# Linear attention with a top-1 mixture of experts: four early expert tiles in place of two, the first with an unsplit fp32 first layer

## The chip, the cores and the metric

The kernel runs on one core of a Trainium2 chip. The metric is the device time of one execution in microseconds (us). The outputs are fp32 and come from fp32 inputs.

## The reference

Four batches of eight heads, 768 positions and 64 channels go through a linear attention that fades with `lam`, one rate a head; its output, seen as 3072 tokens of 512 features, goes through a mixture of eight experts of which each token takes one:

```python
for b in range(nb):                       # blocks of positions, per batch and head
    intra = einsum('bhic,bhjc->bhij', qb, kb) * Dmask
    intra = einsum('bhij,bhjd->bhid', intra, vb)
    inter = einsum('bhid,bhde->bhie', qb * lam_pow, kv_state)
    out[:, :, sl] = intra + inter
    kv_state = lam_block * kv_state + einsum('bhsd,bhse->bhde', kb * rev_pow, vb)
x = out.transpose(0, 2, 1, 3).reshape(3072, 512)
logits = x @ w_gate + modality_bias[modality_id]
e_idx = argmax(logits, axis=1)            # one of 8 experts
gate_w = softmax(logits)[e_idx]
out[mask] = gate_w[mask] * (relu(x[mask] @ w1[e]) @ w2[e])   # 512 -> 1024 -> 512
```

With the inputs used, expert 3 gets 1319 tokens, expert 5 253, expert 6 1494, expert 7 6, and the others none. After the first 1024 tokens the same four have 433, 87, 502 and 2, after the first 2048 they have 885, 164, 994 and 5.

## The kernel before, in words

**The attention.** The positions are taken in chunks of 128: 24 chunks, 6 for each batch, in 12 pairs (loop `for m in range(pairs)`). A pair's q, k and v come in one transfer of 2 MB (`load`, L88 and, for the first two pairs, L92) into one of six slots of 2 MB, which later serve the expert weights too: raw1 and raw2 (w1 and w2 of one expert as they arrive) and w1h, w1l, w2h, w2l (their high and low parts). For each chunk TensorE makes the scores (L253), VectorE masks them (L257), TensorE adds what comes from the state (L292) and from the values (L300), ScalarE copies the result out as xt (L303), VectorE transposes it (`turn`, L309), and a transfer on ScalarE's queue stores the rows in xs in device memory (L313). The state is three rotating tiles: POOL multiplies the old one by the fade (`fade`, L273), TensorE makes the new products kv (L265), VectorE adds both (`add`, L282). After every second pair, the gate matmuls (`gates`, L320) make the logits of four chunks.

**The routing.** It goes in three batches of 8 chunks (1024 tokens): `choose` (L340: the expert of each token, its weight), `ranks` (L364 to L367, matmuls that count each token's place in its expert's list), `slots_of`, and `write_slots` (L394: POOL's indirect transfers that write each token's number into the table inv in device memory). `count` adds up the tokens of each expert. All of the small VectorE instructions of these functions show line 340, that of the helper `put`; they are put on a list, and `do(n)` issues the next n of them.

**The experts.** Tiles of 256 tokens of one expert ("wide"), and two "thin" tiles of 64 and 32 tokens for remainders. `early_list` chooses two full tiles from the first 1024 tokens (listA); the rest follows from `late_list` (listB), with at least MIN_WIDE = 10 wide tiles. For a tile, SP fetches its piece of inv (`fetch_idx`: found, idx, L559 to L567), VectorE makes row indices of it (`spread_idx`, gidx, L575), POOL gathers the rows with indirect transfers (`fetch_rows`, xg, L585), VectorE turns them (`turn_rows`, xt, L610), and ScalarE and VectorE split x and the weights into a high part (L543) and a low part (L544). `fetch_w1` and `fetch_w2` (L600, L605) fetch the weights of the tile's expert in four transfers each. A product of split operands is three F32R matmuls (`three`, L622 to L624). The first layer goes in four blocks of 24 matmuls; after each block ScalarE takes hh (L643) and VectorE hl (L644). The second layer is two halves of 24 matmuls of 512 columns; its result y goes out by an indirect transfer (L658). A thin tile isn't split: its two layers are plain fp32 matmuls (L674 and L701), with transposes between (L685 and L687).

**The order.** TensorE, VectorE, ScalarE and SP issue in the order in which the code is written (`manual_schedule`), and POOL's instructions are chained by `pool()`. The two early tiles begin right behind the attention; the choice of the last 1024 tokens, their ranks, counts and `late_list` are issued between the blocks of tile 0's first layer (`rank_last`) and behind it. Then come the thin tiles, then ten wide ones, for which everything is prepared a tile ahead.

## Time and profile before

| | us |
|---|---|
| median of 3 runs | 445.49 (445.44 to 452.16) |
| the profiled execution | 446.0 |
| its span | 444.2 |
| TensorE matmuls busy | 392.7 (88%) |
| VectorE busy | 263.5 (59%) |
| POOL busy | 222.5 (50%) |
| ScalarE busy | 196.3 (44%) |
| bytes moved | 71.41 MB, mean 161 GB/s |
| mean granted clock of TensorE | 0.947 of full speed |

The profile is of one execution; the times of its stretches are counted from the start of the span. A matmul's record begins when it starts and its end is modelled, so that records of neighbours overlap. PE is TensorE, PEld its weight loads, DVE VectorE, ACT ScalarE, POOL GpSimd, SP the engine that issues most transfers; SPq, ACTq and POOLq stand for instructions that issue a transfer. The shares are means over an attention of some 112 us, two early tiles, two thin tiles and ten late tiles, which differ.

### The profile page before, as it was taken

How to read it: one execution, taken by the hardware profiler on the slowest of the kernel's cores; microseconds unless marked ns; L12 is line 12 of the kernel's file. 1: busy time of each engine (PE TensorE's matmuls, PEld its weight loads, DVE VectorE, ACT ScalarE, POOL GpSimd, SP SyncE). 2: the span in 40 equal slices, each digit the busy share in tenths (PEclk: the TensorE clock that was granted, in tenths of full speed). 3: DMA queues.
4: the chain of work that ended last, by engine and by line, in shares of the span. 5: the costliest groups of instructions: out<-in, count | busy, mean ns of one | idle time of the engine just before them, and what ended most of it. 6: DMA issues, size and time to landing. Idle time of an engine off the chain costs nothing.

```text
span 444.2 us, 9748 instructions
## 1 busy us (share of the span) xinstructions
PE 392.7 (88%) x3532; PEld 344.5 (78%) x3532; DVE 263.5 (59%) x437; ACT 196.3 (44%) x353; POOL 222.5 (50%) x229
## 2 busy tenths in 40 slices
PE   6999998795779973967999999999999999999991
PEld 3889887683678862636988898989898989898980
DVE  5467879677457842035766666666667675748410
ACT  1367452446135410116463636464645455555510
POOL 3664576498748105653282828283737464550100
PEclk8699999899859987989999999999999999999997
DMA  7999999399613153970011216778311112020100
GB/s 254 348 415 408 413 412 409 114 345 327 208 54 96 48 192 73 373 264 26 11 59 39 62 38 189 247 206 260 105 49 45 55 28 73 19 69 3 47 25 23
DMA packets 35129, 71.41 MB, mean 161 GB/s; under 512 B 15353, under 2 KB 15353, under 8 KB 35072
## 3 DMA queue, kind: packets, MB, share of 16 engines
q1 hardware_dynamic: 24304, 51.65, 33.5%
q0 software_dynamic: 5936, 12.69, 8.6%
q10 hardware_dynamic: 4832, 6.36, 3.9%
q8 instruction: 30, 0.49, 0.4%
q14 instruction: 27, 0.22, 0.2%
HBM read 90.95 MB, written 13.67 MB: 236 GB/s over the span
## 4 chain that ended last, share of the span: by engine, by line
issue 39%; POOL 17%; DVE 5%; DMA 5%; another core or an unknown queue 3%; SPq 2%; ACT 1%; POOLq 0%; DVEq 0%; ACTq 0%
POOL xg L585 13%; POOL out_dram L658 4%; DMA both<-in_w_dram 2%; DMA raw<-in_w_dram 2%; DVE w2l L544 1%; DVE w1l L544 1%; DVE hl L644 1%; SPq L600 0%; ACT w1h L543 0%; DMA found<-inv 0%; SPq L567 0%; ACT xh L543 0%; SPq L605 0%; DVE xt L610 0%
## 5 line engine op out<-in xcount | busy, mean ns | idle before, releaser
L585 POOL DMA_INDIRECT xg<-xs,gidx x96 | 115.2, 1200 | 95.0 <-DVE xt L610 66.3
L623 PE MATMUL o<-w2l,hh 128*128 128x512 f32 x192 | 75.7, 394 | 7.6 <-DVE w2l L544 7.6
L544 DVE TENSOR_TENSOR w2l<-raw,w2h 128x1024 fp32r<-128x1024 f32 x48 | 58.7, 1223 | 35.8 <-ACT w2h L543 24.5
L624 PE MATMUL o<-w2h,hl 128*128 128x512 f32 x192 | 75.7, 394 | 0.0
L622 PE MATMUL o<-w2h,hh 128*128 128x512 f32 x192 | 75.2, 392 | 0.0
L622 PE MATMUL kv<-xh,w1h 128*128 128x256 f32 x192 | 56.6, 295 | 5.8 <-DVE hl L644 5.8
L544 DVE TENSOR_TENSOR w1l<-raw,w1h 128x1024 fp32r<-128x1024 f32 x48 | 55.8, 1221 | 4.5 <-ACT w1h L543 1.9
L623 PE MATMUL s<-xl,w1h 128*128 128x256 f32 x192 | 55.6, 289 | 1.1 <-issue 1.1
L624 PE MATMUL s<-xh,w1l 128*128 128x256 f32 x192 | 55.8, 291 | 0.3 <-issue 0.3
L623 PE MATMUL kv<-xl,w1h 128*128 128x256 f32 x192 | 55.7, 290 | 0.0
L624 PE MATMUL kv<-xh,w1l 128*128 128x256 f32 x192 | 55.5, 289 | 0.0
L622 PE MATMUL s<-xh,w1h 128*128 128x256 f32 x192 | 55.4, 288 | 0.0
L543 ACT CAST w2h<-raw 128x1024 fp32r<-128x1024 f32 x48 | 50.0, 1041 | 2.9 <-DVE xn L309 2.9
L623 PEld LDWEIGHTS o<-w2l,hh 128*128 128x128 f32 x192 | 36.4, 190 | 15.3 <-DVE w2l L544 8.0
L243 ACT ACTIVATE kd<-load,dk 128x64 f32<-128x64 f32 x128 | 31.8, 335 | 36.5 <-DMA wgq<-in_wg_dram 10.1
L543 ACT CAST w1h<-raw 128x1024 fp32r<-128x1024 f32 x48 | 46.8, 1046 | 0.7 <-DMA raw<-in_w_dram 0.7
L622 PEld LDWEIGHTS kv<-xh,w1h 128*128 128x128 f32 x192 | 37.8, 197 | 8.0 <-DVE hl L644 7.7
L658 POOL DMA_INDIRECT out_dram<-y,idx x20 | 23.4, 1172 | 40.8 <-ACT y L657 31.4
L624 PEld LDWEIGHTS o<-w2h,hl 128*128 128x128 f32 x192 | 36.4, 190 | 8.0 <-DVE hl L644 0.3
L622 PEld LDWEIGHTS o<-w2h,hh 128*128 128x128 f32 x192 | 36.5, 190 | 7.1
L643 ACT ACTIVATE hh<-kv 128x512 fp32r<-128x512 f32 x24 | 14.4, 598 | 57.0 <-PE kv L624 29.2
L624 PEld LDWEIGHTS s<-xh,w1l 128*128 128x128 f32 x192 | 37.3, 194 | 1.8 <-issue 1.8
(193 smaller groups left out, 668.8 us busy)
## 6 DMA issues: line engine op xcount, KB each, us to landing
raw<-in_w_dram SPq DMA_DIRECT2D x104, 512.0 KB
load<-in_qkv_dram SPq DMA_DIRECT2D x10, 2048.0 KB
xs<-xn ACTq DMA_DIRECT2D x24, 256.0 KB
load<-in_qkv_dram SPq DMA_DIRECT2D x8, 512.0 KB
both<-in_w_dram SPq DMA_DIRECT2D x8, 512.0 KB
xg<-xs,gidx POOLq DMA_INDIRECT x96
inv<-pad SPq DMA_DIRECT2D x2, 388.0 KB
found<-inv SPq DMA_DIRECT2D x48, 8.0 KB
```

The lines of the kernel that those rows point to most:

```text
L243: nc.scalar.activation(out=kds[g][:, p, hl, :], in_=kn[:, p, hl, :], func=AF.Copy, scale=dk[:, hl, p, P - 1 : P])
L543: nc.scalar.copy(out=hi, in_=src)
L544: nc.vector.tensor_tensor(out=lo, in0=src, in1=hi.bitcast(F32), op=ALU.subtract)
L585: pool(nc.gpsimd.indirect_dma_start(out=to[:, t, :], out_offset=None, in_=xs[:rows, :], in_offset=bass.IndirectOffsetOnAxis(ap=gidx[:, t : ...
L622: nc.tensor.matmul(out, ah, bh, start=first, stop=False)
L623: nc.tensor.matmul(out, ah, bl, start=False, stop=False)
L624: nc.tensor.matmul(out, al, bh, start=False, stop=last)
L643: nc.scalar.activation(out=hh[a][:, b], in_=hp, func=AF.Relu)
L644: nc.vector.scalar_tensor_tensor(out=hl[a][:, b], in0=hp, scalar=0.0, in1=hh[a][:, b].bitcast(F32), op0=ALU.max, op1=ALU.subtract)
L658: sc = nc.gpsimd.indirect_dma_start(out=out, out_offset=bass.IndirectOffsetOnAxis(ap=idx[:, t, 0:1], axis=0), in_=y, in_offset=None, bound ...
```

## The change

- Four early tiles: two from listA as before, two from a listB made after 2048 tokens; what remains is listC, and MIN_WIDE is 8. The routing of the second batch is issued at pairs 8 and 11 and in tile 0, that of the last one in tile 1, `late_list` in tile 2, and the thin tiles' indices in tile 3.
- Tile 0's first layer takes raw1 and xt as they are, in plain fp32: 64 matmuls in place of 96, with no split of w1 and x. Its second layer is split as before.
- The indirect transfers of slots and rows are kept as jobs; after a matmul, `tick` takes the next job and makes it wait for that matmul. `go(n)` issues n jobs with no such wait, `need(key)` those that are left of a kind.
- w1 of tile 0 is fetched at pair 6, ahead of the index fetches, which stand at pair 7.
- The first two chunks are computed one after the other. The gate weights come laid out by the host in one transfer, on SP with the modality and the bias ahead of the third pair's load.
- The state is faded within its sum: four scalar_tensor_tensor of 128x64 on VectorE for each chunk, in place of POOL's product and VectorE's addition.

```diff
-EARLY = 2
+SOON = 2
+EARLY = 2 * SOON
-MIN_WIDE = 10
+MIN_WIDE = 8
...
-        pool(nc.gpsimd.memset(wgq, 0.0))
-        for i in range(HB):
-            for r in range(2):
-                nc.scalar.dma_start(out=wgq[halves2[r ^ i], i, :, :E], in_=wg[halves2[r]])
-        nc.scalar.dma_start(out=mod, in_=modality)
-        nc.scalar.dma_start(out=mb, in_=mbias.partition_broadcast(P))
+        nc.sync.dma_start(out=wgq, in_=wg)
+        nc.sync.dma_start(out=mod, in_=modality)
+        nc.sync.dma_start(out=mb, in_=mbias.partition_broadcast(P))
+        load(2)
...
-                nc.vector.tensor_tensor(out=state[(c + 1) % 3], in0=faded.pop(g), in1=kp[:, g % HB], op=ALU.add)
+                for p in range(NP):
+                    nc.vector.scalar_tensor_tensor(out=state[(c + 1) % 3][:, p, :], in0=state[c % 3][:, p, :],
+                                                   scalar=pq[:, p, P - 1 : P], in1=kp[:, g % HB, p, :],
+                                                   op0=ALU.mult, op1=ALU.add)
...
+        def tick(mm):
+
+            if jobs:
+                tc.add_manual_dep(jobs.pop(0)[1]().ins, mm.ins.name,
+                                  mybir.DependencyInfo(mybir.DependencyClass.Sync, mybir.DependencyReason.DATA),
+                                  reason="order")
...
+                        if whole:
+                            mm = nc.tensor.matmul(hp[:, j, :], raw1[:, i, kc, fs], xt2[:, kc, :],
+                                                  start=(kc == 0), stop=(kc == KC - 1))
+                        else:
+                            mm = three(hp[:, j, :], w1h[:, i, kc, fs], w1l[:, i, kc, fs], xh[c][:, d, :], xl[c][:, d, :],
+                                       kc == 0, kc == KC - 1)
+                    if 2 * i + j in ticks:
+                        tick(mm)
...
-            if m == 7:
-                for n in range(EARLY):
-                    fetch_idx(n)
+            if m == 6:
                 raw1 = w1_part("raw1", F32)
                 fetch_w1(*fetch_regs(0, True))
-            elif m == 8:
+            elif m == 7:
+                for n in range(SOON):
+                    fetch_idx(n)
                 raw2 = w2_part("raw2", F32)
                 fetch_w2(*fetch_regs(0, True))
-            elif m == 10:
-                w1l = w1_part("w1l", F32R)
-                for i in range(2):
-                    split(raw1[:, i], w1h[:, i], w1l[:, i])
...
+        def amid2(i):
+            if i == 0:
+                late_list(*early)
+            elif i < 3:
+                do(12)
+            else:
+                do()
+
+        def amid3(i):
+            if i == 0:
+                for n in range(thins, wides + 1):
+                    spread_idx(n)
+                    jobs.extend(row_jobs(n))
+
+        first_layer(amid0, whole=True)
+        need(1)
+        fetch_w1(*fetch_regs(1))
```

What stands in a row on SP behind the last load of q, k and v, before (found: the piece of inv for tile 0; raw: w1 as it arrives):

```order
L88 DMA load<-in_qkv_dram 128x4x1024 x9
L555 TENSOR_LOAD listA
L555 ISA x2
L559 ISA
L559 DMA found_1201<-inv 32x4x16
L559 ISA
L559 DMA found_1201<-inv 32x4x16
```

and now, at the same place:

```order
L88 DMA load<-in_qkv_dram 128x4x1024 x9
L624 TENSOR_LOAD listA
L624 ISA x2
L632 ISA
L632 DMA raw_1102<-in_w_dram 128x1024
L632 ISA
L632 DMA raw_1102<-in_w_dram 128x1024
L632 ISA
L632 DMA raw_1102<-in_w_dram 128x1024
L632 ISA
L632 DMA raw_1102<-in_w_dram 128x1024
L584 TENSOR_LOAD listA
```

The four transfers of w1 for tile 0, which stood behind two index fetches, stand ahead of them.

On VectorE, the end of the long list and what follows it, before (nums: the list's last number; the first layer that follows is tile 1's):

```order
L340 TENSOR_REDUCE many<-wides 1x1
L340 CAST nums<-many 1x1
L544 TENSOR_TENSOR w2l<-raw_1372,w2h 128x1024
L644 SCALAR_TENSOR_TENSOR hl_1774<-s,hh_1772 128x512
L544 TENSOR_TENSOR w2l<-raw_1372,w2h 128x1024
L644 SCALAR_TENSOR_TENSOR hl_1774<-kv,hh_1772 128x512
L544 TENSOR_TENSOR w2l<-raw_1372,w2h 128x1024
L644 SCALAR_TENSOR_TENSOR hl_1775<-s,hh_1773 128x512
L948 TENSOR_LOAD nums
L575 TENSOR_TENSOR gidx_2289<-found_2151,which 128x2
L575 TENSOR_TENSOR gidx_2291<-found_2168,which 128x1
L575 TENSOR_TENSOR gidx_2293<-found_2187,which 128x8
```

and now (the first layer that follows is tile 3's):

```order
L332 TENSOR_REDUCE many<-wides 1x1
L332 CAST nums<-many 1x1
L642 STREAM_TRANSPOSE xt_137<-xg 128x4x4x32 x2
L1024 TENSOR_LOAD nums
L573 TENSOR_TENSOR xl_140<-xt_137,xh_138 128x512
L573 TENSOR_TENSOR xl_141<-xt_137,xh_139 128x512
L573 TENSOR_TENSOR w1l<-raw_1102,w1h 128x1024 x4
L573 TENSOR_TENSOR w2l<-raw_1261,w2h 128x1024
L682 SCALAR_TENSOR_TENSOR hl_1714<-s,hh_1712 128x512
L604 TENSOR_TENSOR gidx_2775<-found_2613,which 128x2
L604 TENSOR_TENSOR gidx_2777<-found_2630,which 128x1
L604 TENSOR_TENSOR gidx_2779<-found_2649,which 128x8
```

The list stood behind the turn and the splits for the next tile; now it stands ahead of them, and the thin tiles' gidx (128x2, 128x1) moved from behind the third block of a first layer to behind the first.

## Rows read from the trace of the kernel before

**Rows 1.** Windows: start:end, length; busy (count) PE, PEld, DVE, ACT, POOL; PEclk, DMA, GB/s.

```profile
0.00:27.00 27.00, 21.92 (x211) 17.19 (x213) 13.06 (x29) 10.42 (x36) 13.82 (x47) 0.81 0.91 321
27.00:80.00 53.00, 50.72 (x1053) 45.60 (x1051) 43.82 (x86) 25.67 (x86) 33.09 (x34) 1.00 1.02 408
...
93.40:112.20 18.80, 13.18 (x210) 10.16 (x209) 13.00 (x18) 8.96 (x18) 15.80 (x16) 0.95 0.95 343
112.20:135.10 22.90, 17.26 (x107) 16.25 (x107) 11.39 (x27) 5.91 (x8) 14.38 (x14) 0.74 0.46 138
135.10:146.10 11.00, 11.00 (x51) 9.08 (x50) 9.01 (x16) 6.12 (x8) 8.78 (x7) 1.00 0.17 55
146.10:162.80 16.70, 13.17 (x98) 12.96 (x97) 12.90 (x63) 6.22 (x8) 1.00 (x1) 0.90 0.44 153
...
183.50:206.20 22.70, 15.65 (x167) 8.98 (x166) 5.20 (x10) 5.23 (x9) 12.29 (x12) 0.92 0.64 229
...
252.00:434.70 182.70, 180.69 (x1150) 163.76 (x1149) 110.48 (x126) 93.07 (x122) 84.16 (x68) 1.00 0.29 91
434.70:444.20 9.50, 0.02 (x1) 0.00 (x0) 0.00 (x0) 0.69 (x1) 0.98 (x1) 0.68 0.07 26
```

**Rows 2.** Waits of PE: what waits <- for what: us in total, times, longest us.

```profile
PE o L623 <- DVE w2l L544: 7.6, 1, 7.6
PE kv L622 <- DVE hl L644: 5.8, 9, 3.5
PE x L364 <- DVE m L340: 4.0, 1, 4.0
PE x L320 <- ACT xt L303: 3.8, 1, 3.8
...
PE x L685 <- ACT xh L543: 2.1, 1, 2.1
```

**Rows 3.** Timeline of ACT, end of the attention: start, us, engine, line, operation [idle <-releaser].

```profile
101.85 2.94 ACT L543 CAST w1h<-raw 128x1024 fp32r<-128x1024 f32 x3 [0.66 <-DMA raw<-in_w_dram]
108.18 0.62 ACT L543 CAST xh<-xt 128x512 fp32r<-128x512 f32 x1 [3.39 <-DVE xt L610]
...
109.22 1.06 ACT L303 COPY xt<-o 128x512 f32<-128x512 f32 x2
```

**Rows 4.** Timeline: POOL's fade, a comparison beside it, the addition, and hl.

```profile
61.05 0.63 POOL L273 TENSOR_TENSOR faded<-state,pq 128x256 f32<-128x256 f32 x1
61.13 1.88 DVE L340 TENSOR_TENSOR geA<-cntA,geA 1x96 f32<-1x96 f32 x1
...
69.74 0.42 DVE L282 TENSOR_TENSOR state<-faded,kv 128x256 f32<-128x256 f32 x1
...
155.92 0.68 DVE L644 SCALAR_TENSOR_TENSOR hl<-s,hh 128x512 fp32r<-128x512 f32 x1
```

**Rows 5.** Timeline of PE: the first thin tile's two layers.

```profile
183.48 3.67 PE L674 MATMUL s<-raw,xf 128*64 128x256 f32 x32
...
195.48 5.36 PE L701 MATMUL o<-raw,hnt 128*64 128x256 f32 x32 [0.78 <-issue]
```

**Rows 6.** Timelines of DVE and SP: turn, split, the long list, the late indices.

```profile
136.58 1.29 DVE L610 STREAM_TRANSPOSE xt<-xg 128x512 f32<-128x512 f32 x2
140.08 4.63 DVE L544 TENSOR_TENSOR w1l<-raw,w1h 128x1024 fp32r<-128x1024 f32 x4 [0.17 <-ACT w1h L543]
...
148.69 0.07 DVE L340 MEMSET start<- 1x1 f32 x2
...
154.67 0.14 DVE L340 CAST nums<-many 1x1 int32<-1x1 f32 x1
...
158.76 1.88 SPq L562 DMA_DIRECT2D found<-inv  x4
...
173.46 0.17 DVE L575 TENSOR_TENSOR gidx<-found,which 128x8 int32<-128x8 int32 x1 [4.50 <-DMA found<-inv]
```

**Rows 7.** Timelines of DVE and SP: the first index, the first fetch of w1.

```profile
84.96 0.17 DVE L575 TENSOR_TENSOR gidx<-found,which 128x8 int32<-128x8 int32 x1 [3.97 <-DMA found<-inv]
...
88.57 2.05 SPq L600 DMA_DIRECT2D raw<-in_w_dram  x4
```

More of the change, by code (lines that the diff above doesn't have):

```diff
@@ L92, in load @@
                     nc.sync.dma_start(out=halves[m][:, part, c], in_=source(m)[:, part, c])
-        for m in range(3):
+        for m in range(2):
             load(m)
@@ new lines, in early_list @@
+            put(nc.vector.tensor_tensor, out=lst[:, 2, 1:], in0=ex[:, 1:], in1=ex[:, : SOON - 1], op=ALU.not_equal)
+            if before is not None:
+                put(nc.vector.tensor_tensor, out=lst[:, 2, 0:1], in0=ex[:, 0:1], in1=exP[:, SOON - 1 :], op=ALU.not_equal)
+            took = const.tile([1, E, SOON], F32, name="took" + nm)
+            sh = [1, E, SOON]
+            put(nc.vector.tensor_tensor, out=took, in0=sidx[:, :E].unsqueeze(2).to_broadcast(sh),
+                in1=taken.unsqueeze(1).to_broadcast(sh), op=ALU.is_equal)
@@ L457, in late_list @@
+            n = const.tile([1, E], F32, name="n" + nm)
+            put(nc.vector.tensor_reduce, out=n, in_=took, axis=AX, op=ALU.add)
+            if before is not None:
+                put(nc.vector.tensor_tensor, out=n, in0=n, in1=nP, op=ALU.add)
+            return ex, n
         def late_list(exA, nA):
-            cnt, n2 = count_tiles(XT + 1, "B")
+            cnt, n2 = count_tiles(XT + 1, "C")
             def per_expert(nm):
@@ L577, in spread_idx, with row_jobs, one @@
             idxs[n].append(gidx.rearrange("p h t -> p (h t)"))
-        def fetch_rows(n, part=None):
+        def row_jobs(n):
             cols = tiles[n][0]
             to = xg if cols == TT else xq[n - EARLY]
-            rows = 4 * RC * P if n < EARLY else 4 * N
+            rows = 4 * RC * P * (n // SOON + 1) if n < EARLY else 4 * N
             gidx = idxs[n][1]
-            for t in range(gidx.shape[-1])[part or slice(None)]:
-                pool(nc.gpsimd.indirect_dma_start(
+            def one(t):
+                return pool(nc.gpsimd.indirect_dma_start(
                     out=to[:, t, :], out_offset=None, in_=xs[:rows, :],
@@ L588, in fetch_rows @@
                     bounds_check=rows - 1, oob_is_err=False))
+            return [(n, lambda t=t: one(t)) for t in range(gidx.shape[-1])]
         def fetch_regs(n, always=False):
@@ L623, in three, with first_layer @@
             nc.tensor.matmul(out, ah, bl, start=False, stop=False)
-            nc.tensor.matmul(out, al, bh, start=False, stop=last)
+            return nc.tensor.matmul(out, al, bh, start=False, stop=last)
         def spare():
             return ps.tile([P, HB, NP, D], F32, name="kv", bufs=1).rearrange("p c a d -> p (c a d)")
-        def first_layer(between=lambda i: None):
+        def first_layer(between=lambda i: None, whole=False, ticks=range(8)):
             for i in range(4):
@@ L815, in linear_attention_moe @@
                 load(m + SLOTS)
+            if m == 4:
+                ranks(routed[-1])
             if m == pairs - 1:
-                split(raw1[:, 3], w1h[:, 3], w1l[:, 3])
+                turn_rows()
             if m > 0:
@@ L900, in linear_attention_moe @@
         fetch_w1(*fetch_regs(thins + 1, True), to=both1)
-        for n in range(thins, wides + 1):
-            fetch_rows(n)
         fetch_idx(wides + 1)
```

312 lines of the change are left out of this document (173 added, 139 removed).

## The prediction

> **What bounds the kernel now.** I read the page first, then the busy time in stretches cut where the matmuls change their kind, then the waits of TensorE, then the timelines around those waits. The profiled execution took 446.0 us: 444.2 of span and 1.8 around it; the median of the three timed runs, 445.49, lies 0.5 lower, so a sum made against the profile is one for the median too.
>
> The reader is to see three regimes in [rows 1]. In the late wide tiles, 252.0 to 434.7, TensorE is busy 180.69 of 182.70 us at clock 1.00: eight tiles, 22.85 us each, bound by TensorE alone. In the attention, 27 to 80, TensorE is busy 50.72 of 53.00 and the DMA engines are full as well (408 GB/s); from 0 to 27 they moved only 321 GB/s. Between 112.2 and 206.2 TensorE loses most: the two early tiles last 112.2 to 183.5, which is 71.3 us or 35.65 each, where a late one needs 22.85, and the clock granted there is 0.74 to 0.90; the two thin tiles (183.5 to 206.2) hold it busy for 15.65 of 22.70.
>
> A first layer of 96 matmuls is a late tile less its second layer, which stands alone from 135.1 to 146.1 with no gap [rows 1]: 22.9 - 11.0 = 11.9 us.
>
> The waits say what the losses hang on [rows 2]: 7.6 on the split of w2, 4.0 on the routing's m before the rank matmuls, 3.8 on ScalarE's copy xt before the last gate matmuls, 2.1 on xh before the thin tile's transposes. All are queues of small work on VectorE and ScalarE that stand ahead of what TensorE wants, not lack of engine time.
>
> **The change part by part.**
>
> a) The start of tile 0, now 112.2. The last gates wait 3.84 us because xt stands on ScalarE behind three casts of w1 and both casts of xh [rows 3]. Tile 0 needs no split of w1 and x any more, so these casts go: -3.8. What is late next is the routing of the last pair, which VectorE does without those subtractions. The last pair's stretch is 18.8 long with 13.18 busy; less the 3.8 it has 1.8 of other idle, which I count as gone: -1.8. At the start, the gate constants leave the four scattered transfers for one, and the first blocks go one by one: the DMA engines lost 27 x (1 - 321/408) = 5.8 us up to 27, and I take half, -3.0 (ends 0 and -5.8). The fade inside the sum replaces one POOL instruction of 0.63 and one VectorE addition of 0.42 [rows 4] by four of 128x64 on VectorE. No row shows the new form: four could take as little as the one addition, 0.42, or 4 x 0.68 = 2.7, the price of a scalar_tensor_tensor of 128x512 [rows 4]. I take 0.2 each, between, as a 128x256 addition of 0.42 is the nearer row: +0.4 for each of 16 chunks = 6.4 us of VectorE, which was busy 43.82 of 53 in this stretch. Mostly hidden, and the detour over POOL goes; I count +1.5 (ends -3 and +10). Sum: 112.2 - 3.8 - 1.8 - 3.0 + 1.5 = 105.1.
>
> By the Trainium skill ("SBUF — State Buffer", section "Who interferes with whom") a VectorE instruction with two SBUF inputs and a GpSimd instruction that reads SBUF lock each other out. A 1x96 comparison that took 1.88 us beside POOL's fade [rows 4] agrees. The new form has one SBUF tensor and one in PSUM, so by that rule the +1.5 would be 0 and the whole sum 1.5 lower.
>
> b) Tile 0. Its first layer is 64 fp32 matmuls of 128x256. No row has one with 128 stationary columns; 32 with 64 columns took 3.67 us [rows 5], two side by side, so 16 passes of 256 columns at 0.23. I take 64 x 0.225 = 14.4 (ends: 11.9, and 64 x 0.42 = 26.9 if a full-width one costs the double). Second layer 11.0, hand-over 0.3: 25.7. The rank matmuls that waited 4.0 now wait beside the same work, but nothing stands between ranks and the choice made at the end of the attention.
>
> c) Tile 1: 22.9, and 2.3 because the matmul that counts tokens now stands behind routing work on VectorE issued in the same first layer, between two blocks: hh, as long as the cast xh of its size, 0.62 [rows 3], hl 0.68 [rows 4], five small routing instructions at 0.16 each (below, d), and 0.2 of hand-over. Then 1.3 for the lower clock behind such a gap: the stretch from 146.1 to 162.8 holds a first layer and the 3.5 us wait on hl, its mean clock is 0.90, and 16.7 - 11.9 - 3.5 = 1.3 [rows 1, 2]. By itself that gives 22.9 + 2.3 + 1.3 = 26.5.
>
> d) Tile 2 carries the long list. Its last 39 instructions ran from 148.69 to 154.81, 6.1 us or 0.16 each [rows 6], and now stand on VectorE behind the last hl and ahead of turning the rows and of the split for tile 3. hl itself is about 4.0 late: two blocks hold w2l (1.2, as w1l), hl 0.7 and 12 list instructions (1.9), 3.8 in a block of 11.9 / 4 = 3.0, so VectorE is 1.6 behind, with w2l 1.2, hl 0.7 and 0.5 of hand-over to go. Then 6.1, the turn 1.3, xh 0.62, two xl as long as hl and 0.1, so 2.1, and the first w1l 1.2 [rows 3, 4, 6]: 14.7, beside a second layer of 11.0. 22.9 + 3.7 + 1.3 = 27.9.
>
> e) Tile 3: the thin tiles' indices. Before, VectorE waited for them inside tile 1: the transfers were issued from 158.76 on and the last gidx ran at 173.46 [rows 6], 14.7 us, and the 7.6 of w2l followed. In the new program the fetch is issued ahead of tile 2's second layer, and gidx stands after the first block of tile 3: 11.0 + 3.0 = 14.0 later. 0.8 for the difference; if w2l is held as long as it was, +3.7. 22.9 + 0.8 = 23.7.
>
> f) Losses that I can't place. From 112.2 to 135.1 a first layer of 11.9 took 22.9: 4.0 the rank wait [rows 2], and 7.0 more that no single wait explains, at a mean clock of 0.74, so for part of it at 1.2 in place of 2.4 GHz. Four early tiles have such work beside them; I take 4.0 in all (ends 0 and 28).
>
> g) Thin tiles: 22.7, less the 2.1 on xh (xh and xt now stand after the thin tiles' first needs), less 1.7: L701 took 5.36 us where L674 needed 3.67 for the same count [rows 5]: 18.9.
>
> h) Eight late tiles instead of ten: 8 x 22.85 = 182.8. i) The end: 9.5, and 1.8 outside the span.
>
> The indirect transfers now wait for a matmul each. They are behind POOL's other work only; the POOL stretch that feeds the late tiles was busy 84.16 of 182.70 [rows 1], so I cost them at nothing there; in the early tiles a late one is part of f.
>
> Sum: 105.1 + 25.7 + 26.5 + 27.9 + 23.7 + 4.0 + 18.9 + 182.8 + 9.5 + 1.8 = 425.9, so 426.0, 4.4% below the median. Against before: attention -7.1, four early tiles with f 107.8 where two took 71.3 (+36.5), thin tiles -3.8, two late tiles fewer -45.7.
>
> **A rule against it.** The fetch of w1 goes ahead of the index fetch on SP. Before, VectorE stood still for 3.97 us until found had landed and gidx ran at 84.96; raw1 was issued behind, at 88.57 [rows 7]. The Trainium skill ("DMA: Bandwidth & Descriptors", section "Queues, rings and completion order") says that a queue's descriptors are consumed in order on each engine, so that found would now land behind the 2.1 MB of w1. No row of before has found behind a big transfer, so the trace neither bears it out nor excludes it. By the rule, 2.1 MB at the 408 GB/s of [rows 1], 5.1 us, less some 3 us by which the slots are now written earlier, an estimate, would hold VectorE 2.1 longer: 428. I don't take it: w1 is asked for a pair of chunks ahead of found, and a pair is some 8 us ((112.2 - 27) / 10.5), more than 5.1.
>
> **The rivals.**
> 1. The attention keeps its length. For it: DMA is full from 27 to 80, so a faster start can be lost there, and VectorE's extra 6.4 us fall in its busiest stretch. Against: the 3.8 of the gates has a plain cause that is removed. Tile 0 then starts at 112.2 + 1.5: 434.5.
> 2. The early tiles run without gaps: the additions in c (3.6), d (5.0), e (0.8) and f (4.0) fall away, 13.4 in all: 412.5. For it: VectorE is busy only about half of any of these stretches [rows 1]. Against: each addition has a queue of its own.
> 3. The early tiles end midway between the old pace and mine, 29.3 each or 117.2 (+9.4), and the attention is unchanged (+8.6): 443.9, no change. For it: the routing work is the same in sum and is only spread over more tiles.
> 4. Slower: the routing chain, which before made two tiles 12.8 us each too long, is now a chain for each list: choice, ranks, slots written, found, gidx, rows, each released by a matmul, so each early tile waits for its rows. If all four run at 35.65, they take 142.6 in place of 107.8: 460.7. It decides (slower than before) from 32.0 per early tile on, (107.8 + 20.1) / 4. Against: tile 3's rows are asked for a whole tile ahead.
> That the early lists would be short of full tiles is excluded: the first 1024 tokens hold 433 and 502 of two experts, the first 2048 hold 885 and 994, 3 + 3 full tiles, and four are asked for.
>
> **How the numbers follow.** Forecast 0.55 (its own range 418 to 436), rival 1 0.15, rival 2 0.10, rival 3 0.13, rival 4 0.07. About 2% (436.6 and 454.4) can be told from no change: faster 0.55 + 0.15 + 0.10 = 0.80, same 0.13, slower 0.07. The range leaves out rival 4 and most of rival 3 above, and goes down to rival 2: 411 to 442.
>
> **What would show it.** In the changed profile: first matmul of the unsplit layer at 105 (112 or later: step a is wrong); that layer 14.4 long, 0.225 a matmul (27: the fp32 price is wrong); no wait of the gates on xt; early tiles of 26 to 28 us, the longest the third; the thin part at 19; eight tiles of 22.85. A wait of TensorE over 5 us on xt, xh or gidx in the early tiles, or POOL transfers that end just ahead of them, would speak for rival 4.

## The result and the profile after

The changed kernel took 423.47 us (median of 4, 421.58 to 425.38), and 0.9506 of the kernel before measured beside it, with a 95% interval of 0.9414 to 0.9598. The forecast was 426.0, range 411 to 442. Two more measurements, on two chips, gave 425.08 (0.9437, 0.9333 to 0.954) and 422.83 (0.9583, 0.9513 to 0.9654). The chips differ: beside four groups of runs the kernel before took 445 to 449 us, beside a fifth, on another chip, 432.5, so a run is compared with runs of its own chip first.

The time falls as forecast, but its parts don't. The profiled execution took 425.38, of which 423.6 are span. The same view as in [rows 1], cut at the changed kernel's stages (start:end, length; busy PE, PEld, DVE, ACT, POOL; granted clock, DMA share, GB/s):

```profile
0.00:27.00 27.00, 20.27 (x225) 16.19 (x229) 17.82 (x43) 8.50 (x28) 15.26 (x46) 0.84 0.91 341
...
110.50:124.60 14.10, 14.10 (x75) 12.29 (x75) 8.62 (x28) 5.63 (x7) 10.59 (x9) 1.00 0.61 181
124.60:135.70 11.10, 11.10 (x50) 9.19 (x49) 9.83 (x26) 6.13 (x8) 6.43 (x6) 1.00 0.77 242
135.70:166.20 30.50, 24.68 (x156) 22.00 (x155) 18.99 (x37) 12.40 (x17) 19.10 (x15) 0.94 0.55 187
166.20:194.70 28.50, 23.19 (x145) 20.33 (x143) 18.86 (x77) 8.96 (x13) 14.39 (x14) 1.00 0.10 30
194.70:220.30 25.60, 24.40 (x146) 21.85 (x146) 13.42 (x18) 10.78 (x14) 15.94 (x14) 0.93 0.45 141
220.30:233.70 13.40, 12.10 (x167) 7.74 (x166) 4.66 (x9) 5.59 (x9) 2.04 (x2) 1.00 0.56 185
233.70:414.10 180.40, 179.15 (x1154) 162.91 (x1152) 115.23 (x130) 94.76 (x124) 86.11 (x72) 1.00 0.28 91
414.10:423.60 9.50, 0.00 (x0) 0.00 (x0) 0.00 (x0) 0.69 (x1) 0.98 (x1) 0.69 0.08 28
```

Tile 0 is the rows from 110.50 to 135.70, then come tiles 1, 2 and 3 with a row each, the thin tiles, the eight late tiles and the end. Against the sum:

| step | forecast | measured |
|---|---|---|
| a, start of tile 0 | 105.1 | 110.5 |
| b, tile 0 | 25.7 | 25.2 (14.1 + 11.1) |
| c, tile 1 | 26.5 | 30.5 |
| d, tile 2 | 27.9 | 28.5 |
| e, tile 3 | 23.7 | 25.6 |
| f, not placed | 4.0 | in the four tiles |
| g, thin tiles | 18.9 | 13.4 |
| h, eight late tiles | 182.8 | 180.4 |
| end, and outside the span | 11.3 | 11.3 |

Against before, the attention gave 112.2 - 110.5 = 1.7 us, the four early tiles cost 109.8 - 71.3 = 38.5 more than the two, the thin tiles gave 22.7 - 13.4 = 9.3, and the late part 228.5 - 180.4 = 48.1. That is 20.6 of span. No run has the four early tiles alone, so this split of the gain is read from the stages of one profile of each kernel. The same view as in [rows 2], of the changed kernel:

```profile
PE kv L654 <- DVE hl L682: 4.3, 3, 1.9
PE x L417 <- DVE ohsum L332: 3.9, 1, 3.9
PE o L284 <- DVE state L269: 3.5, 1, 3.5
PE s L250 <- DVE state L272: 3.4, 1, 3.4
PE s L654 <- ACT w1h L572: 2.8, 1, 2.8
```

The 7.6 on w2l, the 4.0 on m, the 3.8 on xt and the 2.1 on xh of [rows 2] are gone. In their place stand the count (3.9, step c), the split ahead of tile 3 (2.8, step d), and two waits of the attention for the state. The one of 3.4 ends at 22.83, in the new start. The other, 3.5, is for a state that is only a copy, and its cause stands in the timelines of SP and VectorE of the changed kernel:

```profile
73.01 1.74 SPq L632 DMA_DIRECT2D raw<-in_w_dram  x4
78.82 4.14 SPq L588 DMA_DIRECT2D found<-inv  x4
...
87.50 0.17 DVE L604 TENSOR_TENSOR gidx<-found,which 128x8 int32<-128x8 int32 x1 [6.20 <-DMA found<-inv]
...
88.22 0.39 DVE L269 COPY state<-kv 128x256 f32<-128x256 f32 x1
89.14 0.81 DVE L272 SCALAR_TENSOR_TENSOR state<-state,pq,kv 128x64 f32<-128x64 f32 x4
```

VectorE stands for 6.20 us ahead of gidx, which comes at 87.50 where [rows 7] had 84.96, and the copy of the state queues behind it. The last row is the new fade: four in 0.81, the 0.2 each of step a.

### The profile page after: what moved, and what is told of

Same layout as the page of the kernel before. It is cut to its first block, busy times and chain, and to the rows that moved or that the text cites. A ratio compares the mean times of both kernels' runs of the same rounds, so it can differ in the third digit from the quotient of the medians.

```text
span 423.6 us, 9814 instructions
## 1 busy us (share of the span) xinstructions
PE 382.1 (90%) x3501; PEld 336.1 (79%) x3501; DVE 267.4 (63%) x506; ACT 195.7 (46%) x363; POOL 207.0 (49%) x210
## 4 chain that ended last, share of the span: by engine, by line
PE 52%; issue 22%; POOL 9%; DVE 8%; DMA 3%; ACT 1%; SPq 1%; another core or an unknown queue 1%; POOLq 0%; DVEq 0%; ACTq 0%
PE o L654 6%; PE o L656 6%; PE o L655 6%; POOL xg L615 5%; PE s L250 4%; PE s L656 3%; PE kv L656 3%; PE s L654 3%; PE s L655 3%; PE kv L654 3%; PE kv L655 3%; PE o L292 3%; POOL inv L389 2%; PE kv L262 2%; PE o L284 1%
## 5 line engine op out<-in xcount | busy, mean ns | idle before, releaser
L615 POOL DMA_INDIRECT xg<-xs,gidx x96 | 107.6, 1121 | 78.6 <-issue 23.2
L698 POOL DMA_INDIRECT out_dram<-y,idx x24 | 34.7, 1444 | 68.1 <-ACT y L697 51.1
L654 PE MATMUL kv<-xh,w1h 128*128 128x256 f32 x176 | 49.7, 282 | 4.4 <-DVE hl L682 4.3
L654 PE MATMUL s<-xh,w1h 128*128 128x256 f32 x176 | 50.3, 286 | 2.8 <-ACT w1h L572 2.8
L656 PE MATMUL s<-xh,w1l 128*128 128x256 f32 x176 | 50.3, 286 | 0.8 <-DVE w1l L573 0.8
L655 PE MATMUL s<-xl,w1h 128*128 128x256 f32 x176 | 50.0, 284 | 0.0
L655 PE MATMUL kv<-xl,w1h 128*128 128x256 f32 x176 | 49.5, 281 | 0.4 <-issue 0.4
L656 PE MATMUL kv<-xh,w1l 128*128 128x256 f32 x176 | 49.4, 280 | 0.0
L654 PEld LDWEIGHTS o<-w2h,hh 128*128 128x128 f32 x192 | 36.5, 190 | 12.8 <-issue 5.6
L655 PEld LDWEIGHTS o<-w2l,hh 128*128 128x128 f32 x192 | 36.5, 190 | 7.3
L654 PEld LDWEIGHTS s<-xh,w1h 128*128 128x128 f32 x176 | 33.9, 193 | 3.8 <-ACT w1h L572 3.2
L227 POOL TENSOR_TENSOR qd<-load,pq 128x512 f32<-128x512 f32 x20 | 25.3, 1282 | 22.8 <-DMA load<-in_qkv_dram 15.2
```

Source lines behind the costliest of these rows:

```text
L227: pool(nc.gpsimd.tensor_tensor(out=qds[g], in0=loaded(g)[1], in1=pq, op=ALU.mult))
L615: return pool(nc.gpsimd.indirect_dma_start(out=to[:, t, :], out_offset=None, in_=xs[:rows, :], in_offset=bass.IndirectOffsetOnAxis(ap=gidx ...
L654: nc.tensor.matmul(out, ah, bh, start=first, stop=False)
L655: nc.tensor.matmul(out, ah, bl, start=False, stop=False)
L656: return nc.tensor.matmul(out, al, bh, start=False, stop=last)
L698: sc = nc.gpsimd.indirect_dma_start(out=out, out_offset=bass.IndirectOffsetOnAxis(ap=idx[:, t, 0:1], axis=0), in_=y, in_offset=None, bound ...
```

## The experiments

**Order of the fetches.** The index pieces ahead of w1 again, both at pair 7:

```diff
-            if m == 6:
-                raw1 = w1_part("raw1", F32)
-                fetch_w1(*fetch_regs(0, True))
-            elif m == 7:
+            if m == 7:
                 for n in range(SOON):
                     fetch_idx(n)
+                raw1 = w1_part("raw1", F32)
+                fetch_w1(*fetch_regs(0, True))
```

> The changed kernel with the old order of fetches at pair 7: the index pieces first, then w1 of tile 0 (which in the changed kernel goes out at pair 6, at 73.01, and found only at 78.82). Theory 1: found lands behind the 2.1 MB of w1, so VectorE waits 6.20 us for it before gidx (87.50), where it waited 3.97 before (84.96); with the old order that wait falls to 4 us or less, gidx runs 2 to 3 us earlier and tile 0 starts 2 to 4 us before 110.5: about 421 where the changed kernel has 423.5 to 425. Rival 2: found waits for the slots that POOL writes, not for w1, so gidx stays at 87 and the time stays within 1 us. Rival 3: w1, now later, holds up tile 0's first layer: 2 us or more slower.

Measured: 419.1 us (416.81 to 422.71), ratio 0.94 (0.9331 to 0.9468); on the same chip the changed kernel with the old start, below, took 424.94. Its timelines of SP and VectorE:

```profile
76.06 2.74 SPq L588 DMA_DIRECT2D found<-inv  x4
...
81.02 0.17 DVE L604 TENSOR_TENSOR gidx<-found,which 128x8 int32<-128x8 int32 x1 [1.62 <-DMA found<-inv]
...
84.34 1.95 SPq L632 DMA_DIRECT2D raw<-in_w_dram  x4
```

gidx runs at 81.02 in place of 87.50, TensorE's wait of 3.5 for the copied state falls to 0.3, and tile 0 starts at 105.9 in place of 110.5. Theory 1 holds, by more than it said, and the third is out: w1, issued at 84.34, is there in time. The 6.5 us have two parts: found is issued 2.8 earlier here (76.06 against 78.82, where the profile has SP wait for a store of xs), and from its first issue to gidx it takes 5.0 in place of 8.7. Even so the gain is not whole at the end: the thin tiles took 16.4 us here and 13.4 in the changed kernel.

**The fade.** POOL's product and VectorE's one addition again:

```diff
+                faded[g] = work.tile([P, NP, D], F32, name="faded", bufs=1)
+                pool(nc.gpsimd.tensor_tensor(out=faded[g], in0=state[c % 3],
+                                             in1=pq[:, :, P - 1 : P].to_broadcast([P, NP, D]), op=ALU.mult))
...
-                for p in range(NP):
-                    nc.vector.scalar_tensor_tensor(out=state[(c + 1) % 3][:, p, :], in0=state[c % 3][:, p, :],
-                                                   scalar=pq[:, p, P - 1 : P], in1=kp[:, g % HB, p, :],
-                                                   op0=ALU.mult, op1=ALU.add)
+                nc.vector.tensor_tensor(out=state[(c + 1) % 3], in0=faded.pop(g), in1=kp[:, g % HB], op=ALU.add)
```

The edit also leaves the tile lgt one buffer in place of two.

> The changed kernel with the old fade: POOL multiplies, VectorE adds. Theory 1, the prediction's own term: the fade inside the sum costs 0.4 us more of VectorE for each of 16 chunks and 1.5 us on the path, so that undoing it makes the attention 1 to 2 us shorter (tile 0 starts at 108.5 to 109.5). Rival 2: what it gains is the detour over POOL and the time in which POOL and VectorE hold each other up, which is worth more than 0.4 a chunk; undoing it makes the attention 1 to 5 us longer. Rival 3: hidden, within 1 us.

Measured: 427.4 us (423.28 to 430.07), ratio 0.9623 (0.9546 to 0.9701); tile 0 starts at 113.3, which is 2.8 later than in the changed kernel and 2.1 later than in the kernel with the old start on the same chip. Theory 1 falls: the sign was wrong. (In three profiles of the changed kernel tile 0 starts at 110.4 to 110.9, so 2 to 3 us are more than their scatter.) The grouped view of VectorE's instructions shows why in part, first with the old fade:

```profile
L280 DVE TENSOR_TENSOR state<-faded,kv 128x256 f32<-128x256 f32 x16 | 6.6, 410 | 8.2 <-POOL faded L271 6.1 <-PE kv L263 1.8
```

and in the changed kernel:

```profile
L272 DVE SCALAR_TENSOR_TENSOR state<-state,pq,kv 128x64 f32<-128x64 f32 x64 | 13.2, 268 | 4.2 <-remote 3.6 <-PE kv L262 0.5
```

The new form has 13.2 - 6.6 = 6.6 us more work, as costed (6.4), but the additions no longer wait 6.1 us for POOL. The difference of the totals is within what the intervals allow; the stage and the waits agree with rival 2.

**The start.** Four scattered transfers, the third load ahead, chunks 0 and 1 side by side again:

```diff
-        nc.sync.dma_start(out=wgq, in_=wg)
-        nc.sync.dma_start(out=mod, in_=modality)
-        nc.sync.dma_start(out=mb, in_=mbias.partition_broadcast(P))
-        load(2)
+        pool(nc.gpsimd.memset(wgq, 0.0))
+        for i in range(HB):
+            for r in range(2):
+                nc.scalar.dma_start(out=wgq[halves2[r ^ i], i, :, :E], in_=wg[halves2[r]])
+        nc.scalar.dma_start(out=mod, in_=modality)
+        nc.scalar.dma_start(out=mb, in_=mbias.partition_broadcast(P))
...
-        from_state((0,))
-        values(0)
+        scores(1)
+        keys(1)
         products(0)
```

> The changed kernel with the old start: four scattered transfers of the gate weights on ScalarE's queue, the third pair's load ahead of them, the first two chunks side by side. Theory 1, the prediction's term: the new start is worth 3.0 us, so that this one is about 3 us slower all through. Rival 2: the transfers bound the attention after the start (410 GB/s from 27 to 76 in both), pair 1 reads its state at 26.5 where it was 27.5 before, and the gates of pair 1 come at 30.8 in both, so the start is worth 0 to 1 us.

Measured: 424.94 us (421.27 to 425.55), ratio 0.952 (0.9445 to 0.9596); tile 0 starts at 111.2, 0.7 later than in the changed kernel. Rival 2 holds. Up to 27 us the changed kernel moved 341 GB/s and this run 325, so the start did get better. From 27 to 73 both move 411 to 412 GB/s, and nearly all of the gain is gone by tile 0.

**Releasing the indirect transfers.** The same order on POOL with no wait for matmuls:

```diff
-                tc.add_manual_dep(jobs.pop(0)[1]().ins, mm.ins.name,
-                                  mybir.DependencyInfo(mybir.DependencyClass.Sync, mybir.DependencyReason.DATA),
-                                  reason="order")
+                jobs.pop(0)[1]()
```

> The changed kernel with the indirect transfers in the same order on POOL, but none of them made to wait for a matmul. Theory 1, the prediction's: the waits cost nothing and are worth nothing, within 1 us. Rival 2: they spread the transfers, and without them they go out in a row, hold up VectorE and the weight fetches and cost 2 us or more in the early tiles. Rival 3: the waits make the rows of tiles 1 to 3 late; without them it is 1 to 4 us faster.

Measured: 432.51 us in the median of four, but from 424.62 to 432.78, and the one at 424.62 is as short as the changed kernel's; the executions are too far apart for a verdict. What the profiled execution (432.45), one of the three long ones, lost is to be seen in the waits of ScalarE, summed over the span:

```profile
ACT hh L679 <- remote: 23.9, 6, 7.1
...
ACT hh L679 <- issue: 7.1, 5, 1.9
```

"remote" is a release that the profile can't put to anything on this core; not all of such a wait is lost time (last section). In the longest one, ScalarE takes hh at 189.32, 7.1 us after its last work, though the matmuls that it copies were done before, and TensorE waits 5.2 for it; POOL issued indirect transfers in a row up to 188.0. Whether the waits for matmuls prevent this stays open, as not every execution had it.

**The unsplit layer alone**, in the kernel before: two early tiles, tile 0 in fp32, no splits of w1 and x in the attention, tile 1's w1 fetched behind tile 0's first layer.

```diff
+                        if whole:
+                            nc.tensor.matmul(hp[:, j, :], raw1[:, i, kc, fs], xt2[:, kc, :],
+                                             start=(kc == 0), stop=(kc == KC - 1))
+                            continue
...
-                for i in range(2):
-                    split(raw1[:, i], w1h[:, i], w1l[:, i])
...
-        first_layer(rank_last)
+        first_layer(rank_last, whole=True)
+        fetch_w1(*fetch_regs(1))
```

> The kernel before with one part of the change alone: tile 0's first layer unsplit, no splits of w1 and x at the end of the attention, two early tiles and all else as it was. Theory 1, the prediction's: the gates' wait of 3.8 us goes, and tile 0's first layer, which took 22.9 with its waits on the routing, hides the 2.3 us more of matmul time (64 x 0.225 against 96 x 0.124): 3 to 5 us faster than before, 441 to 443. Rival 2: the routing of the last batch is what ends last in that stretch, and it starts no earlier: no change within 1 us. Rival 3: the fetch of tile 1's w1, which now has to wait until tile 0 has used raw1, is late: slower by 2 us or more.

Measured: 453.11 us (448.05 to 457.93), ratio 1.0119 (1.0061 to 1.0177), so some 1% slower, and by none of the three theories: tile 1's w1 isn't what is waited for. Tile 0 starts at 120.7, 8.5 later than before, since the gates wait for xt longer (12.6 in two waits, 3.8 before), with no cast in front of it. The timeline of ScalarE and one window of all engines:

```profile
110.36 0.59 ACT L303 COPY xt<-o 128x512 f32<-128x512 f32 x1 [9.87 <-remote]
118.22 0.59 ACT L303 COPY xt<-o 128x512 f32<-128x512 f32 x1 [7.28 <-remote]
```

```profile
113.00:116.00 3.00, 0.00 (x0) 0.00 (x0) 0.00 (x0) 0.00 (x0) 2.39 (x3) 0.50 0.21 64
```

For three microseconds, of 6.5 in all, TensorE, VectorE and ScalarE do nothing and the DMA engines move 64 GB/s; POOL alone is busy, in a row of indirect transfers that runs from 100.94 to beyond 122. The profile of the run above has such a stretch of 4.5 us (184.8 to 189.3), and that of the kernel before one of 2.3 (last section).

**The waits alone**, in the kernel before: the 24 indirect transfers from the end of the attention to the end of tile 0 released by matmuls.

```diff
-        fetch_rows(1)
-        write_slots(RC)
+        jobs += [lambda t=t: one_row(1, t) for t in range(TT // Q)] + [one_slot] * RC
...
+                        if kc % 2:
+                            tick(mm)
```

> The kernel before with one part of the change alone: from the end of the attention to the end of tile 0, the 24 indirect transfers (the 4 + 4 slots of the second batch, tile 1's 8 rows, the 8 slots of the last batch) each wait for a matmul of tile 0, where POOL issued them in a row before. All else stays, two early tiles and the splits too. Theory 1, from the run without these waits (8 us slower) and the run of the kernel before with the unsplit layer (ScalarE's copy xt late by 9.9 and 7.3 us with no releaser on this core while POOL issued 17 in a row): a row of indirect transfers holds up the other engines. Then the gates' wait of 3.8 and much of the 7.0 that nothing explained in tile 0's first layer go: 5 to 10 us faster, 436 to 441. Rival 2, the prediction's: those losses come from ScalarE's casts and the routing queue on VectorE; no change within 2 us. Rival 3: the slots come later, so that the thin tiles' indices do: slower by 2 us or more.

Measured: 435.17 us (430.81 to 439.84), ratio 1.0046 (1.0014 to 1.0078). It ran on the chip on which the kernel before takes 432.49, and its profile has no "remote" wait on TensorE, VectorE or ScalarE. Theory 1's gain did not come: on this chip the waits cost half a per cent. Whether the kernel before has stalls there that they could prevent isn't known, as it has no profile on that chip. One part of theory 1 is decided even so. The gates still wait 4.0 for xt, with the transfers spread and no stall:

```profile
PE x L320 <- ACT xt L303: 4.0, 1, 4.0
```

That wait is thus not made by these transfers standing in a row, and the prediction's cause for it, the casts on ScalarE, agrees with this run.

**The split layer back**, in the changed kernel:

```diff
             if m == pairs - 1:
                 turn_rows()
+                split_rows()
+                for i in (2, 3):
+                    split(raw1[:, i], w1h[:, i], w1l[:, i])
...
+                for i in range(2):
+                    split(raw1[:, i], w1h[:, i], w1l[:, i])
         store(B * NC - 1)
+        fetch_w1(*fetch_regs(1))
...
-        first_layer(amid0, whole=True)
+        first_layer(amid0)
         need(1)
-        fetch_w1(*fetch_regs(1))
```

> The changed kernel with tile 0's first layer split as the others: w1 and x cast and subtracted at the end of the attention, 96 F32R matmuls in place of 64 fp32 ones, tile 1's w1 fetched ahead of tile 0's first layer. Theory 1, the prediction's: the splits hold up the last gates by 3.8 us, the layer is 2.2 us shorter (14.1 to 11.9): 1 to 2 us slower than the changed kernel. Rival 2: with the indirect transfers out of the way the casts cost the attention less than 2 us, and the split layer is as good or better by up to 2 us. Rival 3: VectorE has to do 4 splits, 2 xl and the routing of the second batch at the same place: 4 us or more slower.

Measured: 418.24 us (417.06 to 418.5), ratio 0.9667 (0.963 to 0.9705), on that same chip, where the changed kernel itself was not run; the total can't be held against it. By its stages, tile 0 starts at 108.6 and takes 14.7 + 11.0, and the gates wait 2.5 for xt, so the casts do cost there. With the unsplit layer and the old order of fetches on the same chip (below) it starts at 103.5 and takes 25.3; 4.6 of these 5.1 are what the order of the fetches gave on another chip. What is left for the unsplit layer is, by this estimate, 1 us or less.

**The count.** Moved behind the first block of tile 2:

```diff
                 jobs.extend([("slots", one_slot)] * RC)
-                count()
 
         def amid2(i):
             if i == 0:
+                count()
                 late_list(*early)
```

> The changed kernel with the matmul that counts the last batch's tokens moved from the end of tile 1's first layer to behind the first block of tile 2's, ahead of the long list that reads it. Theory 1: the 3.9 us that TensorE waits there for the sum of choices, and most of the 1.5 by which the second layer behind it (12.6, clock 0.86) is over 11.0, are a cost of that place alone: tile 1 goes from 30.5 to about 25.5, and nothing takes its place, as the list is not issued before the second block of tile 2; about 418.5. Rival 2: the hl of the last block, which ends only at 152.7 on VectorE, then holds the second layer up, and the gain is 1 us or less.

Measured: 423.38 us (421.67 to 423.9), ratio 0.9386 (0.9317 to 0.9455), against 425.08 of the changed kernel on the same chip. Tile 1 takes 26.5 there, 4 less than in the changed kernel, but tile 3 takes 29.9, where the second run of the changed kernel has 25.6: the third gidx now waits 5.2 for found. From the start of tile 1 to the thin tiles it is 82.1 here and 80.6 there. Rival 2 named the wrong place, but the gain is indeed given back, and the totals (423.38 and 425.08) can't be told apart.

**The long list behind the splits**, as before:

```diff
             elif i < 3:
                 do(12)
-            else:
-                do()
...
-            if i == 0:
+            if i == 2:
...
         split_w1()
+        do()
         for n in range(thins, wides + 1):
```

> The changed kernel with the last part of the long list issued on VectorE behind the turn and the splits for tile 3, as it stood in the kernel before, and the thin tiles' indices spread behind the third block of tile 3 again. Theory 1: the waits ahead of tile 3 (2.8 on w1h, 0.8 on w1l) go and the lower clock behind them too, 4 to 5 us, and the thin tiles' rows still come in time: about 419. Rival 2: the indices come some 7 us later; VectorE waits for found in tile 3, w2l and hl wait behind it, and the gain is given back or more (within 1 us, or up to 4 slower).

Measured: 431.54 us (428.47 to 432.94), ratio 0.9563 (0.9482 to 0.9643), 6.5 slower by the medians than the changed kernel on the same chip. Tile 3 starts 0.1 earlier than there, so theory 1's gain there comes to nothing, and it lasts 31.3 in place of 25.6, and the thin stage behind it 18.3 in place of 13.5. The timeline of VectorE:

```profile
211.26 0.17 DVE L604 TENSOR_TENSOR gidx<-found,which 128x8 int32<-128x8 int32 x1 [5.31 <-DMA found<-inv]
220.16 0.71 DVE L642 STREAM_TRANSPOSE xt<-xg 128x512 f32<-128x512 f32 x1 [6.45 <-DMA xg<-xs,gidx]
228.54 0.71 DVE L642 STREAM_TRANSPOSE xt<-xg 128x512 f32<-128x512 f32 x1 [7.66 <-DMA xg<-xs,gidx]
```

Rival 2 holds, and by more than it said: the list sets when the indices come, and the rows of the first late tile are now waited for as well. Step d's place for the list, with its 2.8 us of wait, is the better one.

**Both together**: the two diffs of the fetches and of the count in one kernel.

> The changed kernel with both edits that shortened a stage by themselves: the index pieces fetched ahead of w1 (tile 0 started at 105.9 in place of 110.5), and the count moved into tile 2 (tile 1 took 26.5 us in place of 30.5, but tile 3 4 us more, from 14.6 to 18.8 in its first layer). Theory 1: the gains add, where the second one is kept only as far as tile 3's wait for the thin tiles' indices lets it: 416 to 419. Rival 2: the gain of the first is eaten by a later wait as well, as the last stage to end is the routing: 420 to 423.

Measured: 413.95 us (412.68 to 417.79), ratio 0.9592 (0.9552 to 0.9632) to 432.49. It is the lowest time of the study, on the chip that is fast for the kernel before too; by its ratio it isn't told apart from the changed kernel, and both theories named absolute times of the other chips. Where before takes some 445 us, the version with the fetches alone has the lowest time, 419.1. Its ratio, 0.94, lies within the interval of the changed kernel's 0.9437, so that it beats the changed kernel is shown by the start of tile 0 and not by the total.

**The changed kernel a third time.**

> The changed kernel a third time, because the kernel before took 445 to 448 us beside the first eight runs and 432.5 beside the last three, so that those three can't be held against the changed kernel's 423.5 and 425.1. Theory 1: the long stalls of the kernel before, in which no engine but POOL works, differ from chip to chip, and the changed kernel, which has few of them, hardly does: where before takes 432 it takes 417 to 422 (ratio 0.965 to 0.975), and where before takes 445 it takes 421 to 425 (0.944 to 0.955). Rival 2: a fast chip is fast for both: 411 and 432, ratio 0.95 anywhere.

Measured: 422.83 us (420.62 to 426.34), ratio 0.9583 (0.9513 to 0.9654), with before at 446.75 on that chip. It came on none of the chips of the other experiments, so neither theory is decided. Tile 0 starts at 110.4, and the stages are the first profile's within 1.2 us but for tile 2, which takes 24.2 in place of 28.5 (24.5 in the second measurement).

## Why the prediction was right, and where not

The total was right to 0.6%, and by the stages the cause named for it held: two late tiles and their 45.7 us go, and the four early ones cost less than that more (forecast 36.5, measured 38.5). That is some 10 of the 20.6 us; the attention was to give 7.1 and gave 1.7, and the thin tiles 3.8 and gave 9.3. The steps in which the sum was wrong cancelled, which was luck: +5.4 in a, +2.0 in b to f, -5.5 in g, -2.4 in h.

- **Step a** failed most, 105.1 against 110.5. It costed the fetch of w1 ahead of the index pieces at nothing ("I don't take it"), since a pair is longer than w1's transfer. The runs showed 6.20 us of wait and 4.6 of path. The estimate that it set aside, 2.1 on top of 3.97, was right for the wait, but the old order would have left only 1.62 of it, so the path lost more than 2.1. The Trainium skill ("DMA: Bandwidth & Descriptors", section "Queues, rings and completion order") says that on each DMA engine a queue's descriptors are consumed in order. The trace agrees, with gidx at 87.50 behind w1 and at 81.02 ahead of it. What the step left out is that w1 shares the DMA engines with what is still in flight, so that its 5.1 us are not what it takes: from its issue on they are full for 9.5 us (the last number is GB/s):

```profile
73.01:82.50 9.49, 9.49 (x215) 8.61 (x208) 8.30 (x17) 7.49 (x28) 1.52 (x2) 1.00 1.03 409
```

  Whether the order in the queue or the full engines make more of found's longer way isn't told apart. With the old order tile 0 starts at 105.9, near the forecast 105.1, but that too is luck, as two of the other terms were off by 2.3 and by about 4 (the next two points).
- The new start was taken at -3.0, "half" of the 5.8; it gave 0.7. Rival 1 had named the full transfers from 27 on, in which a faster start can be lost.
- The fade was taken at +1.5. Its size on VectorE was right (6.4, measured 6.6), its sign on the path wrong: about -2 to -3, the wait for POOL. The sum named the detour over POOL that goes but gave it no price of its own; only the lower end, -3, allowed for it.
- The casts: the 3.8 us of the gates are gone, but tile 0 with its splits put back waits 2.5 for xt and starts no later than the other order of fetches explains. The unsplit layer was worth 1 us or less by that estimate, and alone in the kernel before it brought nothing. Its price in step b, 14.4, was right: 14.1.
- **Step c**: the wait for the count is where it was said, 3.9 in place of 2.3 (2.3 and 3.9 in the two other profiles, for the same first layer of 17.9); with it come hl (1.9), which the sum did not have, and a second layer of 12.6 at a mean clock of 0.86, so for part of it at 1.2 in place of 2.4 GHz, after TensorE's 3.9 us of idle time. Tile 1, not tile 2, is the longest. Mended alone, the wait is given back in tile 3.
- **Step d** was right in kind: TensorE waits 2.8 for w1h and 0.8 for w1l, 3.6 against 3.7. In size it is one profile's: in the two others w1h is waited for 2.0 and 1.7, and tile 2 takes 24.5 and 24.2 against the forecast of 27.9.
- **Step e**: 25.6 against 23.7; w2l no longer waits, the excess lies behind the gap ahead of tile 3, where the clock is down (0.88 over its first layer of 14.6, 0.93 over the tile).
- **Step f**, 4.0, stood for 6.0: the four tiles took 109.8, and b to e had 103.8. The 7.0 of the kernel before that it could not place are, by [rows 1], 17.26 of matmuls where 11.9 suffice, so 5.4 at the lower clock, and the rest of some 1.6 is gaps of TensorE without a named releaser.
- **Step g** failed to the other side, 18.9 against 13.4. It took away two waits (2.1 and 1.7) of a stage in which TensorE idled 7 us. Two more stand in the timeline of the kernel before, a slow pass on `both` (the weights of the second thin tile) and a wait for hnt:

```profile
189.99 1.91 PE L674 MATMUL s<-both,xf 128*32 128x256 f32 x26 [0.58 <-DMA both<-in_w_dram]
204.08 2.23 PE L701 MATMUL o<-both,hnt 128*32 128x128 f32 x64 [2.88 <-DVE hnt L687]
```

  The changed kernel has neither:

```profile
220.29 3.67 PE L714 MATMUL s<-raw,xf 128*64 128x256 f32 x32
223.89 1.93 PE L714 MATMUL s<-both,xf 128*32 128x256 f32 x32
225.76 0.66 PE L725 MATMUL x<-ident,hn 128*128 128x128 f32 x4
227.20 3.67 PE L741 MATMUL o<-raw,hnt 128*64 128x256 f32 x32 [0.79 <-DVE hnt L727]
```

  The two passes over the weights take 5.5 us together, where they took 10.6 (183.48 to 194.04) before: some 3 of that is the pass on `both`, 2.1 the wait on xh that the sum had. The wait for hnt, which is one of the stops of the last section, falls from 2.88 to 0.5. The first `both` is issued 9.4 us ahead of the stage (210.93), where it was 6.2 before (177.30); that this is why the pass runs through is argued, not shown.
- **Step h**, 182.8 against 180.4: in seven of the eight late tiles that the price was taken from, TensorE waits 0.24 to 0.32 for hl, and a first layer with that wait takes 12.0, without it 11.5. The changed kernel's take 11.4 and have no such wait; only its first late tile is longer, 24.1.

Some readings in the prediction are off without weight for the sum. Its 29.3 in rival 3 is midway between 35.65 and a late tile's 22.85; midway to its own 26.95 would be 31.3, so 451.9, still no change. The clock "0.74 to 0.90" of the early tiles leaves out the 1.00 from 135.1 to 146.1. The bound of 0.42 for a full-width matmul is not double 0.23.

Rival 1 (the attention keeps its length) came near: 110.5 where before had 112.2. Its total did not come. Rival 4 (every early tile at the old pace) didn't come: the longest took 30.5, and 31.6 in the third measurement.

## What to carry to other kernels

Before a big transfer is moved up a queue, look at which small transfer stands behind it and which in-order engine waits for that: here 2.1 MB of weights, early by one pair of chunks, went with an index that came 6.5 us later, and 4.6 on the path. Price an edit that takes a step off another engine by the waits on both sides of the step, not by its instructions alone. When a step is made early enough to hide, take its whole chain of waits out of the sum, and when one wait is mended, ask which wait of the same chain is next: the count and the list each only moved it.

## What the runs showed of the hardware that was not expected

One loss of the kernel before has no releaser in its rows. In the summed waits of its ScalarE:

```profile
ACT hh L643 <- remote: 27.8, 9, 4.1
...
ACT yn L705 <- remote: 9.3, 1, 9.3
```

and in those of the changed kernel:

```profile
ACT hh L681 <- issue: 5.8, 4, 1.9
...
ACT hh L681 <- remote: 2.3, 1, 2.3
```

The sums, 37.1 us against 2.3, are not what was lost. Eight of the ten waits, 23.7 us, lie in the late tiles, where TensorE works on (180.69 of 182.70 in [rows 1]) and loses some 0.5 each (step h), 4.0 in all. Of the other two, one of 4.1 is in tile 0, where TensorE's gaps without a named releaser come to 1.5, and one of 9.3 in the thin tiles, where TensorE works on until 201.2 and then waits 2.88 for hnt. That makes some 8 us.

At the worst TensorE, VectorE and ScalarE stop at once, beside a row of POOL's indirect transfers: for 6.5 us in the kernel before with the unsplit layer (111.7 to 118.2), 4.5 in the run without waits for matmuls, 2.3 in the kernel before (201.2 to 203.6). Behind the start, the three profiles of the changed kernel have one stretch of 0.8 us or more in which all three stop, and it ends with the index found. The sums of ScalarE's "remote" waits are 0 to 8.3 in all versions of the changed kernel whose transfers wait for matmuls, 23.9 without these waits, and 45.8 in the kernel before with the unsplit layer.

Such rows alone don't do it. The run with the waits alone leaves the thin and the late tiles as they were, and POOL issues the same transfers there in the same rows. Even so its profile has no "remote" wait on ScalarE, its late first layers take 11.5, its longest wait for hnt is 0.8, and its thin stage takes 17.9 in place of 22.7. It ran on the chip on which the kernel before takes 432.49, some 13 us less than elsewhere. So the stalls differ from chip to chip or from one execution to the next, which isn't told apart. What stops the engines isn't shown, nor whether the waits for matmuls prevent it, nor how much of the change's gain is owed to it.

A second one is smaller: an instruction of two elements on VectorE took 3.15 us beside POOL's work, where its like takes 0.2, in the timeline of the changed kernel:

```profile
67.32 0.95 POOL L389 DMA_INDIRECT inv<-pay,sloti  x1 [0.30 <-issue]
67.50 0.15 DVE L332 TENSOR_TENSOR atA<-atA,sidx 1x2 f32<-1x2 f32 x1
67.69 3.15 DVE L332 TENSOR_SCALAR atA<-atA 1x2 f32<-1x2 f32 x1
68.29 2.51 POOL L227 TENSOR_TENSOR qd<-load,pq 128x512 f32<-128x512 f32 x2
```

It begins beside an indirect transfer of POOL and ends when POOL's two products do, 70.8. The Trainium skill ("SBUF — State Buffer", section "Who interferes with whom") lists tensor_scalar among the VectorE instructions that can contend with GpSimd. The row agrees in so far as the instruction is held until POOL is done.

The comparison of [rows 4] that took 1.88 us ends in the same way with a product, and not with the fade, which was over at 61.68. The timeline of POOL in the kernel before:

```profile
61.05 0.63 POOL L273 TENSOR_TENSOR faded<-state,pq 128x256 f32<-128x256 f32 x1
61.63 1.27 POOL L230 TENSOR_TENSOR qd<-load,pq 128x512 f32<-128x512 f32 x1
```

The comparison runs from 61.13 to 63.01, so it is held by the product qd as well, which the changed kernel still has.
